# Half of a first-product sum goes through ScalarE into another PSUM bank, in 16 steps of a fused attention and FFN kernel

## The chip, the cores and the metric

The kernel runs on one core of a Trainium2 chip. The metric is device time in microseconds of one execution; the time given is the median of three runs. A core has TensorE (PE, matrix products, which write only to the accumulator memory PSUM), VectorE (DVE), ScalarE (ACT), GpSimd (POOL) and the queue engine SyncE (SP). Each engine works through its own list of instructions in the order in which the list is written, and waits at an instruction until what it needs from other engines has been signalled. PSUM has 8 banks, each of 128 partitions by 512 float32 values.

## What is computed

For each of B=4 batches, with q, k, v of 6080 x 256 values, a channel attention is computed, and on its output a feed-forward layer with an ELU:

```python
qn = q / (np.linalg.norm(q, axis=1, keepdims=True) + 1e-06)
kn = k / (np.linalg.norm(k, axis=1, keepdims=True) + 1e-06)
s = kn.transpose(0, 2, 1) @ qn / tau
a = softmax over the last axis of s          # 256 x 256 for each batch
x = (v @ a).reshape(24320, 256)
h = x @ w_in                                 # w_in: 256 x 2048
g = np.where(h > 0.0, h, np.exp(np.minimum(h, 0.0)) - 1.0)
out = g @ w_out                              # w_out: 2048 x 256
```

w_in and w_out come as float64.

## The kernel before

Since v @ a @ w_in = v @ (a @ w_in), the kernel forms W' = a @ w_in once for each batch (`wp_item`, tiles `wp`), so that two products are left for each piece of tokens: h = v W' (the first product) and out = g w_out (the second). To keep float32 accuracy on a faster matrix format, each operand is split into a high part and a low part, and each product is made of three matmuls: high x high, high x low, low x high.

The tokens lie along the columns. A batch has 6080 tokens in NB=12 chunks, eight of 512 and then four of 496, 48 chunks in all (numbered 0 to 47). The hidden dimension of 2048 is cut into FT=16 tiles f of 128. One **step** is one pair (chunk c, tile f). Chunks 0 to 3 go first in an interleaved order (64 steps); from chunk M=4 on, step 64 + (c - 4) x 16 + f is (c, f). Chunks 8 to 11, the last four of batch 0, are steps 128 to 191, with 496 columns each.

`take(i)` writes the instructions of step i:

- `h_item` (L416): the first product for step i, into `ph`, a PSUM tile of tag `w`. The contraction of 256 runs as KT=2 halves kt=0 and kt=1, three matmuls each (L423, L424, L425): six matmuls that add up in one bank.
- `elu` (L428): for odd f ScalarE makes a Relu of the negative and an exponential (L434, L435), and VectorE combines (L436); for even f ScalarE makes the exponential alone (L438) and VectorE does two operations (L439, L440). Both forms read `ph`.
- `split_g` (L443) for step i-1: ScalarE casts the high part of g, VectorE subtracts for the low part (L114, L115, the helper `split`).
- `out_item` (L455) for step i-3 (LAG = 3): the second product, six matmuls L461, L463, L465 for each of two output tiles, into the two tiles `po` of the chunk, which sum over all 16 f. Between them stand the matmuls of the next batch's q-k product (`gram`, L203 and L210) in some steps.
- after the last f of a chunk `store` (L468): ScalarE copies each `po` to SBUF (L487), and a DMA goes out on SP's queue (L489).
- side work: squares, casts and sums for the next batch's rows (L181, L114, L182; while batch 0 runs they are written behind steps 127, 131, 135 and so on to 159, among others), norms (step 166), the softmax, and the next batch's W' (`wp_item`).

**PSUM.** The 8 banks are given out by tag: `gram` 2, `w` WB=3 (`ph`, `pn`, `pt`, `pw`), and `o` 8 - KT - WB = 3 (the `po` tiles, two for each chunk). A tile holds its bank until the last instruction that uses it is done; the next tile of the tag waits for a free bank.

**What sets the order.** The framework traces the program and a planner writes each engine's list ahead of the run. Up to step 67 (`in_order`, L554 to L862) TensorE, VectorE and ScalarE are under a manual schedule: their lists have the order of the code. From then on the planner orders the instructions itself, with the order of the code as priority. Instructions in `side` are put behind the step's `elu` on their engine (`issue_after`).

Of the kernel before, what the change touches and what calls it, by code (L numbers as in the profile page):

```python
# [7 lines left out]
F32 = mybir.dt.float32  # L8
# [19 lines left out]
def in_turns(cols):  # L28

    if len(cols.shape) == 3:  # L30
        return cols.rearrange("p x (a b) -> p x b a", a=2)
    return cols.rearrange("p (a b) -> p b a", a=2)
# [22 lines left out]
def channel_attention_then_elu_ffn(ctx: ExitStack, tc, q, k, vT, tau, w_in, w_out, outT):  # L55
# [8 lines left out]
    nc = tc.nc  # L64
# [4 lines left out]
    P = 128  # L69
    KT = C // P  # L70
    FT = F // P
    DT = D // P
    CH = 512
# [14 lines left out]
                pieces.append((c, lo, lo + Q))  # L88
    WB = 3

    LINE = 2048
# [5 lines left out]
    ps = ctx.enter_context(tc.tile_pool(name="ps", bufs=4, space=bass.MemoryType.PSUM))  # L99
# [3 lines left out]
    ones_r = lead_pool.tile([P, P], F32R, name="ones_r")  # L103
# [7 lines left out]
    wo = const.tile([P, FT, 2, D], F32R, name="wo")  # L111
# [273 lines left out]
    def span(c):  # L385

        b, x = divmod(c, NB)
        return b, b * N + sum(sizes[:x]), sizes[x]
# [25 lines left out]
    wps = {}  # L414

    def h_item(c, f, vt):  # L416
        b, _, n = span(c)
        wp = wps[b]
        ph = ps.tile([P, CH], F32, tag="w", bufs=WB, name="ph")
        fs = slice(f * P, f * P + P)  # L420
        for kt in range(KT):
            hi, lo = (in_turns(vt[:, kt, x, 0:n]) for x in range(2))
            nc.tensor.matmul(ph[:, 0:n], wp[kt][:, 0, fs], hi, start=(kt == 0), stop=False)  # L423
            nc.tensor.matmul(ph[:, 0:n], wp[kt][:, 0, fs], lo, start=False, stop=False)  # L424
            nc.tensor.matmul(ph[:, 0:n], wp[kt][:, 1, fs], hi, start=False, stop=(kt == KT - 1))  # L425
        return ph

    def elu(c, ph, both):  # L428
        n = span(c)[2]
        e = work.tile([P, CH], F32, tag="e", bufs=3, name="e")  # L430
        ev, pv = e[:, 0:n], ph[:, 0:n]

        if both:
            nc.scalar.activation(ev, pv, AF.Relu, scale=-1.0)  # L434
            x = nc.scalar.activation(ev, ev, AF.Exp, scale=-1.0)  # L435
            y = nc.vector.scalar_tensor_tensor(ev, ev, -1.0, pv, op0=ALU.add, op1=ALU.max)  # L436
        else:
            x = nc.scalar.activation(ev, pv, AF.Exp)  # L438
            nc.vector.tensor_scalar(ev, ev, 1.0, -1.0, op0=ALU.min, op1=ALU.add)  # L439
            y = nc.vector.tensor_tensor(ev, pv, ev, op=ALU.max)  # L440
        return e, x, y

    def split_g(c, e):  # L443
        n = span(c)[2]
        g = work.tile([P, 2, CH], F32R, tag="g", bufs=4, name="g")
        split(g[:, 0, 0:n], g[:, 1, 0:n], e[:, 0:n])
        return g

    def first(c, f):
        return f == 0 or (c, f) in [(x, lo) for x, lo, _ in pieces]  # L450

    def last(c, f):
        return f == FT - 1 or (c, f) in [(x, hi - 1) for x, _, hi in pieces]

    def out_item(c, f, g, po, between):  # L455

        n = span(c)[2]
        hi, lo = (in_turns(g[:, x, 0:n]) for x in range(2))
        for dt in range(DT):
            o, ds = po[dt][:, 0:n], slice(dt * P, dt * P + P)  # L460
            nc.tensor.matmul(o, wo[:, f, 0, ds], hi, start=first(c, f), stop=False)  # L461
            next(between, None)
            nc.tensor.matmul(o, wo[:, f, 1, ds], hi, start=False, stop=False)  # L463
            next(between, None)
            nc.tensor.matmul(o, wo[:, f, 0, ds], lo, start=False, stop=last(c, f))  # L465
            next(between, None)

    def store(c, f, po):  # L468
        _, t0, n = span(c)
        ov = outT[:, t0 : t0 + n].rearrange("(k p) t -> p k t", p=P)  # L470
        if c < M:
            o = half[c]
        else:
            o = work.tile([P, DT, CH], F32, tag="o", bufs=1, name="o")
        for dt in range(DT):
            y, x = quarters(o[:, dt, 0:n]), quarters_of_turns(po[dt][:, 0:n])
            if c < M and (c, 0, f + 1) not in pieces:
                nc.vector.tensor_add(y, y, x)  # L478
            elif c == NCH - 1 and dt == DT - 1:

                m = n // 2
                nc.scalar.copy(y, x)
                nc.sync.dma_start(ov[:, dt, 0:m], o[:, dt, 0:m])
                nc.scalar.dma_start(ov[:, dt, m:n], o[:, dt, m:n])
                continue
            else:
                nc.scalar.copy(y, x)  # L487
            if f == FT - 1:
                nc.sync.dma_start(ov[:, dt], o[:, dt, 0:n])  # L489
# [53 lines left out]
    wi64, wo64, vraw, vts = {}, {}, {}, {}  # L543
    state = {}
# [228 lines left out]
    for b in range(1, B):  # L773
# [33 lines left out]
        for g in range(NG):  # L807
            x = s0 + length * g // NG
# [5 lines left out]
        x = s1 - FT - 6  # L814
# [18 lines left out]
    def take(i):  # L833

        if i < len(steps):
            c, f = steps[i]
            ph = h_item(c, f, vts[c])
            es[i], *done[:] = elu(c, ph, i < M * FT or f % 2 == 1)
        if 0 <= i - 1 < len(steps):
            gs[i - 1] = split_g(steps[i - 1][0], es.pop(i - 1))  # L840
        j = i - LAG
        if j >= 0:
            c, f = steps[j]
            if first(c, f):

                tag, bufs = ("o", 8 - KT - WB)
                if (c, f) in [piece[0:2] for piece in pieces[-2::-2]]:
                    tag, bufs = ("gram", KT)
                pos[c] = [ps.tile([P, CH], F32, tag=tag, bufs=bufs, name=f"po_{c}_{dt}") for dt in range(DT)]
            out_item(c, f, gs.pop(j), pos[c], fine.pop(i, iter(())))  # L850
            if last(c, f):
                store(c, f, pos.pop(c))
        for fn in loose.get(i, ()):
            fn()
        with tc.issue_after(done[0].ins), tc.issue_after(done[1].ins):
            for fn in side.get(i, ()):
                fn()

    done = []
    for i in range(M * FT + LAG):  # L860
        take(i)
    in_order.close()  # L862
    for i in range(M * FT + LAG, len(steps) + LAG):
        take(i)
# [31 lines left out]
```

## Time and profile before

| | |
|---|---|
| median of 3 runs | 2165.83 us |
| lowest, highest run | 2165.37, 2166.81 us |
| span of the profiled execution | 2163.4 us |
| granted TensorE clock, mean | 1.000 |
| idle before ScalarE's output copies L487, all 11 times | 5.4 us |
| start of step 128 in the trace (first matmul of chunk 8) | 409.38 us |
| start of step 132 | 420.85 us |

The profile comes from one execution, and its span runs from the first to the last instruction. In a timeline each row is start in us, duration in us, engine, line, operation, output <- inputs, shapes, and in brackets how long the engine had been idle and who released it. Matmuls overlap in the array: a duration of 0.37 us belongs to one whose successor starts 0.21 us later, so the spacing of the starts is what a matmul costs. PEld rows are weight loads, which run beside the matmul before. In a row of groups, the number behind x is the count, then come busy time and mean ns, then idle time before the group and its releasers.

### The profile page before, as it was taken

How to read it: one execution, taken by the hardware profiler on the slowest of the kernel's cores; microseconds unless marked ns; L12 is line 12 of the kernel's file. 1: busy time of each engine (PE TensorE's matmuls, PEld its weight loads, DVE VectorE, ACT ScalarE, POOL GpSimd, SP SyncE). 2: the span in 40 equal slices, each digit the busy share in tenths (PEclk: the TensorE clock that was granted, in tenths of full speed). 3: DMA queues.
4: the chain of work that ended last, by engine and by line, in shares of the span. 5: the costliest groups of instructions: out<-in, count | busy, mean ns of one | idle time of the engine just before them, and what ended most of it. 6: DMA issues, size and time to landing. Idle time of an engine off the chain costs nothing.

```text
span 2163.4 us, 27196 instructions
## 1 busy us (share of the span) xinstructions
PE 2158.6 (100%) x10240; PEld 1911.9 (88%) x10240; DVE 1527.0 (71%) x2358; ACT 1469.1 (68%) x2422; POOL 3.3 (0%) x11
## 2 busy tenths in 40 slices
PE   9999999999999999999999999999999999999999
PEld 8888888899888888889988888888998888888998
DVE  7987777778766776776776677667776666666665
ACT  6877777667666666666766666666776666666665
POOL 0000000000000000000000000000000000000000
PEclk9999999999999999999999999999999999999999
DMA  9320222221111111111111112111112000000000
GB/s 357 107 78 30 78 69 68 68 65 49 59 38 50 49 59 49 59 58 46 39 59 39 49 50 68 49 58 49 56 31 67 20 30 27 23 20 11 20 10 20
DMA packets 62532, 120.77 MB, mean 56 GB/s; under 512 B 6208, under 2 KB 16064, under 8 KB 62400
## 3 DMA queue, kind: packets, MB, share of 16 engines
q1 hardware_dynamic: 62256, 118.91, 16.6%
q8 instruction: 80, 1.31, 0.2%
q14 instruction: 52, 0.43, 0.1%
q10 hardware_dynamic: 144, 0.13, 0.0%
HBM read 92.01 MB, written 27.00 MB: 55 GB/s over the span
## 4 chain that ended last, share of the span: by engine, by line
PE 100%; ACT 0%; DVE 0%; issue 0%
PE po L465 15%; PE po L463 15%; PE ph L423 15%; PE po L461 15%; PE ph L424 15%; PE ph L425 15%; PE gram L203 3%; PE gram L549 2%; PE gram L210 1%; PE pw L374 1%; PE pw L373 1%; PE pw L375 1%; PE pe L549 0%; PE pw L370 0%; PE pd L222 0%; PE pt L337 0%
## 5 line engine op out<-in xcount | busy, mean ns | idle before, releaser
L114 ACT CAST g<-e 128x512 fp32r<-128x512 f32 (+1 forms) x768 | 469.6, 611 | 483.5 <-DVE e L440 281.6
L115 DVE TENSOR_TENSOR g<-e,g 128x512 fp32r<-128x512 f32 (+1 forms) x768 | 525.6, 685 | 323.0 <-ACT g L114 295.6
L465 PE MATMUL po<-g,wo 128*128 128x512 f32 (+1 forms) x1536 | 579.3, 377 | 0.0
L463 PE MATMUL po<-g,wo 128*128 128x512 f32 (+1 forms) x1536 | 579.2, 377 | 0.0
L461 PE MATMUL po<-g,wo 128*128 128x512 f32 (+1 forms) x1536 | 578.9, 377 | 0.0
L423 PE MATMUL ph<-vt,wp 128*128 128x512 f32 (+1 forms) x1472 | 555.4, 377 | 0.0
L425 PE MATMUL ph<-vt,wp 128*128 128x512 f32 (+1 forms) x1472 | 554.5, 377 | 0.0
L424 PE MATMUL ph<-vt,wp 128*128 128x512 f32 (+1 forms) x1472 | 554.5, 377 | 0.0
L436 DVE SCALAR_TENSOR_TENSOR e<-e,ph 128x512 f32<-128x512 f32 (+1 forms) x416 | 283.2, 681 | 242.5 <-ACT e L435 241.9
L434 ACT ACTIVATE e<-ph 128x512 f32<-128x512 f32 (+1 forms) x416 | 246.6, 593 | 129.1 <-PE ph L425 114.4
L461 PEld LDWEIGHTS po<-g,wo 128*128 128x128 f32 x1536 | 290.3, 189 | 37.9 <-DVE scr L478 0.2
L463 PEld LDWEIGHTS po<-g,wo 128*128 128x128 f32 x1536 | 290.3, 189 | 37.8
L465 PEld LDWEIGHTS po<-g,wo 128*128 128x128 f32 x1536 | 290.7, 189 | 34.8 <-DVE g L115 0.3
L424 PEld LDWEIGHTS ph<-vt,wp 128*128 128x128 f32 x1472 | 278.2, 189 | 36.2
L425 PEld LDWEIGHTS ph<-vt,wp 128*128 128x128 f32 x1472 | 278.2, 189 | 36.1
L423 PEld LDWEIGHTS ph<-vt,wp 128*128 128x128 f32 x1472 | 278.2, 189 | 36.1
L435 ACT ACTIVATE e<-e 128x512 f32<-128x512 f32 (+1 forms) x416 | 261.3, 628 | 12.6
L440 DVE TENSOR_TENSOR e<-ph,e 128x512 f32<-128x512 f32 (+1 forms) x352 | 240.6, 684 | 10.4
L438 ACT ACTIVATE e<-ph 128x512 f32<-128x512 f32 (+1 forms) x352 | 207.9, 591 | 31.1 <-PE ph L425 29.2
L439 DVE TENSOR_SCALAR e<-e 128x512 f32<-128x512 f32 (+1 forms) x352 | 147.0, 418 | 20.7 <-ACT e L438 20.6
L182 DVE TENSOR_TENSOR acc<-acc,sq 128x1024 f32<-128x1024 f32 x84 | 102.6, 1221 | 12.2 <-ACT sq L181 11.1
L203 PE MATMUL gram<-qk 128*128 128x512 f32 x268 | 101.6, 379 | 0.0
(134 smaller groups left out, 1183.1 us busy)
## 6 DMA issues: line engine op xcount, KB each, us to landing
raw<-in_q_dram SPq DMA_DIRECT2D x76, 256.0 KB, 2.7
raw<-in_k_dram SPq DMA_DIRECT2D x76, 256.0 KB, 3.0
v<-in_v_dram SPq DMA_DIRECT2D x32, 512.0 KB, 3.6
out_dram<-o SPq DMA_DIRECT2D x56, 256.0 KB, 2.1
v<-in_v_dram SPq DMA_DIRECT2D x16, 496.0 KB, 3.5
out_dram<-o SPq DMA_DIRECT2D x31, 248.0 KB, 2.1
wraw<-w_scr SPq DMA_DIRECT2D x12, 512.0 KB, 3.2
room<-in_q_dram SPq DMA_DIRECT2D x16, 256.0 KB, 5.2
```

The costliest lines, as they stand in the source:

```text
L114: nc.scalar.copy(hi, src)
L115: nc.vector.tensor_sub(lo, src, hi.bitcast(F32))
L423: nc.tensor.matmul(ph[:, 0:n], wp[kt][:, 0, fs], hi, start=(kt == 0), stop=False)
L424: nc.tensor.matmul(ph[:, 0:n], wp[kt][:, 0, fs], lo, start=False, stop=False)
L425: nc.tensor.matmul(ph[:, 0:n], wp[kt][:, 1, fs], hi, start=False, stop=(kt == KT - 1))
L434: nc.scalar.activation(ev, pv, AF.Relu, scale=-1.0)
L435: x = nc.scalar.activation(ev, ev, AF.Exp, scale=-1.0)
L436: y = nc.vector.scalar_tensor_tensor(ev, ev, -1.0, pv, op0=ALU.add, op1=ALU.max)
L440: y = nc.vector.tensor_tensor(ev, pv, ev, op=ALU.max)
L461: nc.tensor.matmul(o, wo[:, f, 0, ds], hi, start=first(c, f), stop=False)
L463: nc.tensor.matmul(o, wo[:, f, 1, ds], hi, start=False, stop=False)
L465: nc.tensor.matmul(o, wo[:, f, 0, ds], lo, start=False, stop=last(c, f))
```

## The change

In chunks 8 to 11, for f = 0, 4, 8 and 12 (16 steps), `h_item_seeded` takes the place of `h_item`. The three matmuls of kt=0 go into a tile `first_half` of tag `w`. ScalarE copies it into another bank, `seeded`, of tag `o`, and the three matmuls of kt=1 add to what the copy left there (no `start`). `seeded` is one tile for all 16 steps. Ahead of the first of them one matmul of ones with 512 columns of the weights is written into it. `elu` then reads `seeded` in place of `ph`. All other steps are as before.

```diff
+    SEEDED = (8, 12)
...
+    def h_item_seeded(c, f, vt):
+        b, _, n = span(c)
+        wp = wps[b]
+        if "seeded" not in state:
+            state["seeded"] = ps.tile([P, CH], F32, tag="o", bufs=8 - KT - WB, name="seeded")
+            nc.tensor.matmul(state["seeded"], ones_r, wo[:, 0].rearrange("p x d -> p (x d)"), start=True, stop=True)
+        first_half = ps.tile([P, CH], F32, tag="w", bufs=WB, name="first_half")
+        ph = state["seeded"]
+        fs = slice(f * P, f * P + P)
+        for kt in range(KT):
+            hi, lo = (in_turns(vt[:, kt, x, 0:n]) for x in range(2))
+            to, begin = (first_half, True) if kt == 0 else (ph, False)
+            end = kt == 0
+            nc.tensor.matmul(to[:, 0:n], wp[kt][:, 0, fs], hi, start=begin, stop=False, skip_group_check=not begin)
+            nc.tensor.matmul(to[:, 0:n], wp[kt][:, 0, fs], lo, start=False, stop=False, skip_group_check=not begin)
+            nc.tensor.matmul(to[:, 0:n], wp[kt][:, 1, fs], hi, start=False, stop=True, skip_group_check=not begin)
+            if kt == 0:
+                nc.scalar.copy(ph[:, 0:n], first_half[:, 0:n])
+        return ph
...
             c, f = steps[i]
-            ph = h_item(c, f, vts[c])
+            item = h_item_seeded if SEEDED[0] <= c < SEEDED[1] and f % 4 == 0 else h_item
+            ph = item(c, f, vts[c])
```

## The prediction, made before the changed kernel was run

> **What bounds the kernel now.** I read the page's span, busy shares and chain first, then the windows, then the timeline around steps that the change touches.
>
> ```profile
> span 2163.4 us, 27196 instructions
> ...
> PE 2158.6 (100%) x10240; PEld 1911.9 (88%) x10240; DVE 1527.0 (71%) x2358; ACT 1469.1 (68%) x2422; POOL 3.3 (0%) x11
> ...
> PEclk9999999999999999999999999999999999999999
> ...
> PE 100%; ACT 0%; DVE 0%; issue 0%
> ```
>
> TensorE is busy for 2158.6 of 2163.4 us, its clock is full in every slice, and the chain that ended last is made of matmuls. The three timed runs have their median at 2165.83 us, 2.43 us above the span of the profiled execution; I carry that difference over unchanged. So two things can move the time: the number of matmuls, and gaps between them. The other engines matter only where TensorE waits for them.
>
> ```profile
> 64.00:230.00 166.00, 166.00 (x771) 145.12 (x770) 140.37 (x201) 131.40 (x221) 0.00 (x0) 1.00 0.17 60
> ...
> 420.85:515.00 94.15, 94.15 (x466) 85.25 (x464) 69.64 (x105) 64.03 (x107) 0.68 (x1) 1.00 0.20 66
> ```
>
> These rows of the windows view give, after the length, the busy time of PE, weight loads, DVE, ACT and POOL, then clock, DMA share and GB/s. The second lies in the changed chunks: PE is busy all of it, ACT 64.03 of 94.15 us (68%).
>
> **The step, as it runs now.** The first product of step i is six matmuls (kt=0: L423, L424, L425; kt=1: the same), then six of the second product for step i-3. This is the timeline of step 136 (chunk 8, f=8), one of the 16:
>
> ```profile
> 431.69 1.04 ACT L181 ACTIVATE sq<-raw 128x1024 f32<-128x1024 f32 x1
> ...
> 432.20 0.37 PE L423 MATMUL ph<-vt,wp 128*128 128x496 f32 x1
> ...
> 432.62 0.37 PE L425 MATMUL ph<-vt,wp 128*128 128x496 f32 x1
> ...
> 432.64 1.03 ACT L114 CAST qk<-raw 128x1024 fp32r<-128x1024 f32 x1
> ...
> 432.83 0.37 PE L423 MATMUL ph<-vt,wp 128*128 128x496 f32 x1
> ...
> 433.46 0.37 PE L461 MATMUL po<-g,wo 128*128 128x496 f32 x1
> ...
> 433.57 0.60 ACT L114 CAST g<-e 128x496 fp32r<-128x496 f32 x1
> ...
> 434.08 0.57 ACT L438 ACTIVATE e<-ph 128x496 f32<-128x496 f32 x1
> ...
> 434.71 0.37 PE L423 MATMUL ph<-vt,wp 128*128 128x496 f32 x1
> ```
>
> Columns are start, duration, engine, line. Matmuls of 496 columns start 0.21 us apart. The kt=0 half's last matmul starts at 432.62, the kt=1 half follows at 432.83, the second product takes 433.46 to 434.71.
>
> **What the change adds.** Matmuls: the six stay six, with the same columns. One is new, once: `ones_r` times 512 columns, 0.22 us. Copies: 16 on ScalarE. Waits: the fourth matmul of a changed step needs the copy, and the copy needs the third matmul. Nothing is removed from TensorE, no DMA is added, SP's and POOL's queues are untouched. The nearest rows for the copy are those of the output copies, which read a PSUM bank and follow a matmul:
>
> ```profile
> L487 ACT COPY o<-po 128x496 f32<-128x496 f32 (+1 forms) x8 | 4.6, 575 | 1.0 <-PE po L465 0.9
> ```
> ```profile
> 416.91 0.59 ACT L487 COPY o<-po 128x512 f32<-128x512 f32 x1
> ...
> 417.47 0.38 PE L465 MATMUL po<-g,wo 128*128 128x512 f32 x1
> ...
> 417.89 0.59 ACT L487 COPY o<-po 128x512 f32<-128x512 f32 x1 [0.39 <-PE po L465]
> ...
> 418.94 0.37 PE L461 MATMUL po<-g,wo 128*128 128x496 f32 x1
> ...
> 420.11 0.37 PE L461 MATMUL po<-g,wo 128*128 128x496 f32 x1
> ```
>
> A copy takes 0.58 us; an idle ScalarE starts it 0.42 us after the start of the matmul it waits for (417.47 to 417.89). For the way back, this is an early step in which TensorE waits for VectorE:
>
> ```profile
> 65.55 0.68 DVE L115 TENSOR_TENSOR g<-e,g 128x512 fp32r<-128x512 f32 x1
> ...
> 66.28 0.19 PEld L465 LDWEIGHTS po<-g,wo 128*128 128x128 f32 x1 [0.30 <-DVE g L115]
> 66.28 0.48 PE L465 MATMUL po<-g,wo 128*128 128x512 f32 x1
> ...
> 66.60 0.38 PE L461 MATMUL po<-g,wo 128*128 128x512 f32 x1
> ```
>
> VectorE ends at 66.23, the weights load 0.05 us later, and the next matmul starts 0.32 us after the waiting one instead of 0.22: a wait that is felt costs 0.10 us more, because the weights were not loaded ahead.
>
> **Cost with nothing put in between.** With ScalarE free: 0.42 + 0.58 + 0.05 + 0.10 - 0.21 = 0.94 us of gap. In step 136 ScalarE is not free: the square (431.69) and the cast of rows (432.64) come from step 135 and hold it until 433.57, where the copy could start in place of the cast of g. It ends at 434.15, TensorE goes on at 434.20 where it now does at 432.83, and 0.10 for the weights makes 1.47 us. By the code, such row work is issued in steps 127, 131, ... 159, each just ahead of a changed step: 9 of the 16 pay 1.47, the other 7 pay 0.94. That is 13.2 + 6.6 = 19.8 us, the upper end.
>
> **What can hide it.** In step 136 six matmuls of the second product are ready meanwhile: their g is three steps old. Put in front of the kt=1 half they fill 432.83 to 434.08; one matmul of step 137's first product fills the slot to 434.29, later than 434.20. Nothing is left. With ScalarE free the copy ends at 433.62 and four of the six suffice. This is decided ahead of the run, by the order in which the planner writes TensorE's list, so I look for signs that it reorders. The first 67 steps stand under a manual order, the rest do not:
>
> ```profile
> 99.83 0.60 ACT L434 ACTIVATE e<-ph 128x512 f32<-128x512 f32 x1 [0.55 <-PE ph L425]
> 100.45 0.63 ACT L435 ACTIVATE e<-e 128x512 f32<-128x512 f32 x1
> 100.99 0.60 ACT L114 CAST g<-e 128x512 fp32r<-128x512 f32 x1
> ```
> ```profile
> 436.17 0.58 ACT L434 ACTIVATE e<-ph 128x496 f32<-128x496 f32 x1 [1.51 <-PE ph L425]
> 436.65 0.60 ACT L114 CAST g<-e 128x496 fp32r<-128x496 f32 x1
> 437.17 0.61 ACT L435 ACTIVATE e<-e 128x496 f32<-128x496 f32 x1
> ```
>
> The code writes L434, L435 and then L114. The manual part keeps that; the later part puts the cast between the two, at a point where it was ready and L435 was not. So ready work does overtake in the changed region. On TensorE I find no overtaking, but nothing there was ever blocked: this is the weak link. How good is the planned order in fact?
>
> ```profile
> 389.71 0.38 PE L425 MATMUL ph<-vt,wp 128*128 128x512 f32 x1
> ...
> 390.52 0.62 ACT L114 CAST g<-e 128x512 fp32r<-128x512 f32 x1 [2.01 <-DVE e L440]
> ...
> 391.05 0.59 ACT L434 ACTIVATE e<-ph 128x512 f32<-128x512 f32 x1
> ```
>
> L434 could have run at 389.71 + 0.42 = 390.13, yet ScalarE sat until 390.52 for a cast put first. The plan expected that cast at least 0.39 us sooner than it came. That is the largest such miss that I found. A plan that expects the copy too early puts too few matmuls in between, and TensorE waits for the difference plus 0.10. I take 0.10 us for each of the 16 steps, the price of a wait that is only just felt: some steps will have none, some a little more. The ends are 0 and 19.8 us.
>
> **The other edits.** The seeded bank is one of the three of tag `o`, held over chunks 8 to 11, so a new chunk's sums must wait until the old ones are copied out. The rows above cover that: the copies end at 417.50 and 418.48, the new sums start at 418.94 and 420.11, 1.44 and 1.63 us later. Cost 0; without that cover it is what the copies run late. The changed step's sum is complete later by up to 1.5 us, so g is late too:
>
> ```profile
> 437.29 0.68 DVE L115 TENSOR_TENSOR g<-e,g 128x496 fp32r<-128x496 f32 x1 [0.67 <-ACT g L114]
> ```
> ```profile
> 442.38 0.38 PE L465 MATMUL po<-g,wo 128*128 128x496 f32 x1
> ```
>
> Step 136's g is complete at 437.97 and its second part is first used at 442.38, 4.4 us of cover. Cost 0. Behind the copy in ScalarE's queue stand the cast of the step before and this step's exponential; 16 x 0.58 = 9.3 us on an engine that is 68% busy fits into its gaps. The tight place is the norms of batch 1, in step 167:
>
> ```profile
> 527.73 0.67 DVE L115 TENSOR_TENSOR g<-e,g 128x496 fp32r<-128x496 f32 x1
> ```
> ```profile
> 529.05 0.37 PE L465 MATMUL po<-g,wo 128*128 128x496 f32 x1
> ```
>
> There 0.65 us lie between 528.40 and 529.05, and step 168's copy may come ahead of that cast: 0.58 us, just covered.
>
> **The sum.** 0.22 + 16 x 0.10 = 1.8 us. Span 2163.4 + 1.8 = 2165.2; time 2165.83 + 1.8 = 2167.6 us.
>
> **Rivals.**
> Strict order: the planner leaves the kt=1 half right behind the copy's wait. 19.8 + 0.22 = 20.0 us, 2185.8 us. For it: in all steps of before TensorE's list is in the code's order. Against it: ScalarE's list is not. It decides from the point where fewer than four matmuls stand between the halves. The Trainium skill, TensorE: Matmul & The Clock Gate, section "Step-by-step: what each phase is for", says that TensorE itself pulls only weight loads ahead and keeps matmuls in program order. By that the chip would not repair a strict list, and the time would be this rival's; the wait at 66.28, with ready matmuls behind it, agrees.
>
> Plan too early everywhere: each step has the miss of 0.39 and the 0.10. 16 x 0.49 + 0.22 = 8.1 us, 2173.9 us.
>
> Banks: at the four chunk changes under the hold the output copy slips behind a changed copy, a square and a cast, 0.58 + 1.04 + 1.03 - 1.44 = 1.21 us each; with the 1.8, 6.6 us, 2172.4 us. Against it: no changed copy is issued in the same step as an output copy.
>
> Clock: the short gaps make the granted clock drop to half for the changed steps. Sixteen steps of 94.15 / 33 = 2.85 us (the window holds about 33 steps) would double: 45.6 us, 2211.4 us. Against it: with the wait at 66.28 the window 64 to 230 still reads 1.00. The same page of the Trainium skill, section "A second HAM failure mode: psum-queue depth-cycling", tells of short idle spells between groups of matmuls that made the clock swing between half and full; the trace shows none.
>
> That the second half overwrites the copy instead of adding to it would change the output, not the time: the same columns are written.
>
> Faster: TensorE has one matmul more and no gaps to lose, so only scatter remains.
>
> **How the numbers follow.** Nearly hidden 0.70 (2165.5 to 2170); plan too early 0.12; strict 0.12; banks 0.03; clock 0.01; faster 0.02. A change of 0.2% (4.3 us) is about what a measurement of this kernel tells from none. So same 0.70, slower 0.28, faster 0.02. The range 2164.8 to 2175 takes in the first two cases and the banks, 0.85.
>
> **What would show it.** Right: between the third and fourth first-product matmul of a changed step stand four to eight others, starts stay 0.21 us apart, ACT has 16 copies of about 0.58 us, the clock stays 1.00. Wrong: the fourth follows the third directly with a gap near 1 us and the copy as releaser (strict); gaps of 0.3 to 0.5 us with the same releaser (plan too early); gaps at the first sums of chunks 8 to 11 (banks).

## The result, and the profile after

| | before | after |
|---|---|---|
| median | 2165.88 us (18 runs) | 2169.88 us (18 runs) |
| lowest, highest | 2165.37, 2166.81 us | 2169.12, 2170.98 us |
| span of the profiled execution | 2163.4 us | 2168.0 us |

The ratio is 1.0018, with a 95% interval from 1.0011 to 1.0026: 4.0 us slower, just under the 0.2% that the prediction set as the bound of no change. The forecast was 1.8 us more. The interval leaves out 1: these runs do tell the 4.0 us from nothing, though the prediction reckoned that 0.2% is about what a measurement can tell.

These are the lines of the page after that answer to those shown of before. Lines of the code moved: the kt=0 half of a changed step is L443 to L445 on the tile `first_half`, its kt=1 half L443 to L445 on `seeded`, the copy L447, the second product L483, L485 and L487, the cast of `split` L116.

```profile
span 2168.0 us, 27209 instructions
...
PE 2161.1 (100%) x10241; PEld 1910.5 (88%) x10241; DVE 1529.6 (71%) x2358; ACT 1477.4 (68%) x2438; POOL 3.2 (0%) x11
...
PEclk9999999999999999999999999999999999999999
...
PE 97%; ACT 2%; issue 1%; DVE 0%; DMA 0%; SPq 0%; ACTq 0%
```

One matmul and 16 instructions of ScalarE more, the same full clock. The chain is no longer TensorE's alone: ACT has 2% and "issue" 1%. That share is not the loss, which is 0.2% of the span: where the chain goes back through a copy, it counts the square and the cast ahead of it too. The busy share hides the gaps, since it still reads 100%. The view of the tile `seeded` says who waits (here: duration min/median/max in ns, then first and last start):

```profile
L447 ACT COPY seeded<-first_half x16: 557/562/574, 411.0 to 586.1; 128x496 f32<-128x496 f32 x16
L443 PE MATMUL seeded<-vt,wp x16: 372/477/477, 411.6 to 586.8; 128*128 128x496 f32 x16
...
  ACT seeded L447: 6.9, 21
```

The 16 copies take 0.56 us each. The first matmul behind a copy lasts 0.477 us in the median instead of 0.372, the mark of a wait that is felt, as at 66.28 before. The last row sums the idle time of PE and of its weight queue behind the copy, so it counts some stretches twice.

Step 136 after, the one worked out in the prediction, in the timeline:

```profile
432.90 1.04 ACT L183 ACTIVATE sq<-raw 128x1024 f32<-128x1024 f32 x1
...
433.83 0.37 PE L445 MATMUL first_half<-vt,wp 128*128 128x496 f32 x1
...
433.85 1.03 ACT L116 CAST qk<-raw 128x1024 fp32r<-128x1024 f32 x1
...
434.04 0.37 PE L483 MATMUL po<-g,wo 128*128 128x496 f32 x1
...
434.79 0.56 ACT L447 COPY seeded<-first_half 128x496 f32<-128x496 f32 x1
434.88 0.37 PE L485 MATMUL po<-g,wo 128*128 128x496 f32 x1
...
435.40 0.19 PEld L443 LDWEIGHTS seeded<-vt,wp 128*128 128x128 f32 x1 [0.54 <-ACT seeded L447]
435.40 0.48 PE L443 MATMUL seeded<-vt,wp 128*128 128x496 f32 x1 [0.15 <-ACT seeded L447]
435.51 0.19 PEld L444 LDWEIGHTS seeded<-vt,wp 128*128 128x128 f32 x1
435.71 0.37 PE L444 MATMUL seeded<-vt,wp 128*128 128x496 f32 x1
```

The planner did reorder: five matmuls of the second product stand between the halves (434.04 to 434.88). The sixth came behind (a step's second product is six matmuls in all, three for each output tile). TensorE was free for the next at 434.88 + 0.21 = 435.09; the copy ended at 435.35 and the matmul started at 435.40. That is 0.31 us, and 0.10 more up to the next start (435.71 instead of 435.61). A step without row work ahead, later in the same trace:

```profile
537.06 0.37 PE L445 MATMUL first_half<-vt,wp 128*128 128x496 f32 x1
...
537.47 0.56 ACT L447 COPY seeded<-first_half 128x496 f32<-128x496 f32 x1 [0.65 <-PE first_half L445]
...
537.89 0.37 PE L483 MATMUL po<-g,wo 128*128 128x496 f32 x1
...
538.10 0.45 PE L443 MATMUL seeded<-vt,wp 128*128 128x496 f32 x1
...
538.39 0.37 PE L444 MATMUL seeded<-vt,wp 128*128 128x496 f32 x1
```

Here ScalarE was idle, the copy began 0.41 us after its matmul, four matmuls filled the time, and only 0.08 us were lost, to the weights (538.39 - 538.10 = 0.29 instead of 0.21).

By the spacing of the starts, the 16 steps lose: 9 behind row work 0.34 to 0.42 us each, 3.64 us together; 6 others 0.08 to 0.09 each, 0.48 us; step 168, which got ten matmuls in between, nothing. With the matmul of ones (0.22, and 0.02 at its border) that makes 4.4 us. The runs say 4.0, the spans 4.6.

### The profile page after: what moved, and what is told of

It reads as the page before. It is cut to its first block, busy times and chain, and to the rows that moved or that the text cites. A ratio compares the mean times of both kernels' runs of the same rounds, so it can differ in the third digit from the quotient of the medians.

```text
span 2168.0 us, 27209 instructions
## 1 busy us (share of the span) xinstructions
PE 2161.1 (100%) x10241; PEld 1910.5 (88%) x10241; DVE 1529.6 (71%) x2358; ACT 1477.4 (68%) x2438; POOL 3.2 (0%) x11
## 4 chain that ended last, share of the span: by engine, by line
PE 97%; ACT 2%; issue 1%; DVE 0%; DMA 0%; SPq 0%; ACTq 0%
PE po L487 15%; PE ph L425 15%; PE ph L427 15%; PE ph L426 15%; PE po L485 15%; PE po L483 15%; PE gram L205 2%; PE gram L571 2%; PE gram L212 1%; PE pw L377 1%; PE pw L375 1%; PE pw L376 1%; ACT sq L183 1%; PE pe L571 0%; ACT qk L116 0%
## 5 line engine op out<-in xcount | busy, mean ns | idle before, releaser
L116 ACT CAST g<-e 128x512 fp32r<-128x512 f32 (+1 forms) x768 | 469.5, 612 | 483.6 <-DVE e L462 282.9
L487 PE MATMUL po<-g,wo 128*128 128x512 f32 (+1 forms) x1536 | 579.3, 377 | 0.0
L485 PE MATMUL po<-g,wo 128*128 128x512 f32 (+1 forms) x1536 | 579.2, 377 | 0.0
L483 PE MATMUL po<-g,wo 128*128 128x512 f32 (+1 forms) x1536 | 578.9, 377 | 0.0
L425 PE MATMUL ph<-vt,wp 128*128 128x512 f32 (+1 forms) x1440 | 543.5, 377 | 0.0
L427 PE MATMUL ph<-vt,wp 128*128 128x512 f32 (+1 forms) x1440 | 542.6, 377 | 0.0
L426 PE MATMUL ph<-vt,wp 128*128 128x512 f32 (+1 forms) x1440 | 542.6, 377 | 0.0
L456 ACT ACTIVATE e<-ph 128x512 f32<-128x512 f32 (+1 forms) x416 | 246.6, 593 | 120.0 <-PE ph L427 105.3
L483 PEld LDWEIGHTS po<-g,wo 128*128 128x128 f32 x1536 | 290.3, 189 | 37.9 <-DVE scr L500 0.2
L485 PEld LDWEIGHTS po<-g,wo 128*128 128x128 f32 x1536 | 290.3, 189 | 37.8
L487 PEld LDWEIGHTS po<-g,wo 128*128 128x128 f32 x1536 | 290.7, 189 | 34.7 <-DVE g L117 0.3
L426 PEld LDWEIGHTS ph<-vt,wp 128*128 128x128 f32 x1440 | 272.2, 189 | 35.5
L427 PEld LDWEIGHTS ph<-vt,wp 128*128 128x128 f32 x1440 | 272.2, 189 | 35.5
L425 PEld LDWEIGHTS ph<-vt,wp 128*128 128x128 f32 x1440 | 272.2, 189 | 35.4
L462 DVE TENSOR_TENSOR e<-ph,e 128x512 f32<-128x512 f32 (+1 forms) x336 | 230.1, 685 | 10.2
L460 ACT ACTIVATE e<-ph 128x512 f32<-128x512 f32 (+1 forms) x336 | 198.6, 591 | 28.3 <-PE ph L427 26.5
```

What stands on the lines that cost most here:

```text
L116: nc.scalar.copy(hi, src)
```

## The experiments

The theory to test: the whole cost is TensorE's wait for the copy, and what hides it is only the number of matmuls that the list puts in between. The rivals: the copies as load on ScalarE, the bank taken from tag `o`, or the place of the steps in the kernel. Ratios are to the kernel before on the same chip (2165.67 us for e1 to e4, 2165.76 us for e5 to e8).

| experiment | median, us | over before, us | ratio, 95% interval |
|---|---|---|---|
| e1, list as written | 2186.03 | 20.36 | 1.0093 (1.0078 to 1.0109) |
| e8, before, list as written | 2165.80 | 0.04 | 1.0001 (0.9992 to 1.0010) |
| e4, copy of the whole sum | 2165.79 | 0.12 | 1.0000 (0.9992 to 1.0009) |
| e2, behind the second product | 2167.77 | 2.10 | 1.0010 (1.0001 to 1.0018) |
| e5, behind the next first product | 2166.08 | 0.32 | 1.0001 (0.9992 to 1.0010) |
| e3, two steps later | 2169.18 | 3.51 | 1.0016 (1.0007 to 1.0025) |
| e7, squares on VectorE | 2168.42 | 2.66 | 1.0013 (1.0004 to 1.0021) |
| e6, row work in halves | 2169.88 | 4.12 | 1.0019 (1.0011 to 1.0028) |

The intervals reach about 2 us to either side (3 in e1). By their times e1, e4 and e5 stand clear of the changed kernel; e2, e3 and e7 are told from it by the gaps in their traces alone. By the spacing of the starts the 16 steps lose 4.1 us in the changed kernel, 1.7 in e2, 3.2 in e3, 2.3 in e7, 4.0 in e6, and nothing in e4 and e5; the matmul of ones adds 0.24 to each.

### e1: the list as the code writes it

```diff
+    with tc.manual_schedule(engines={nc.tensor.engine}):
+        for i in range(M * FT + LAG, M * FT + 9 * FT):
+            take(i)
-    for i in range(M * FT + LAG, len(steps) + LAG):
+    for i in range(M * FT + 9 * FT, len(steps) + LAG):
         take(i)
```

> TensorE's list keeps the order of the code over steps 67 to 207, so nothing stands between the two halves of a changed step. Theory (the cost is TensorE's wait for the copy, and only what the planner put in between hides it): 9 steps behind row work wait 1.47 us each and 7 wait 0.94 us, with the matmul of ones 20.0 us over before, 2185.9 us, ratio 1.009. Rival (the 4 us of the change come from the 16 copies as load on ScalarE, the held bank or the matmul of ones, not from the wait): 2169.9 us as with the change.

It took 20.36 us more. Step 136 in its timeline:

```profile
436.48 0.37 PE L445 MATMUL first_half<-vt,wp 128*128 128x496 f32 x1
...
437.38 0.56 ACT L447 COPY seeded<-first_half 128x496 f32<-128x496 f32 x1
...
437.99 0.48 PE L443 MATMUL seeded<-vt,wp 128*128 128x496 f32 x1 [1.14 <-ACT seeded L447]
```

Nothing stands between the halves, and the next start comes 1.51 us after the third matmul instead of 0.21. The six ready matmuls of the second product stand behind the waiting one and do not pass it. That is the rule of the Trainium skill (TensorE: Matmul & The Clock Gate, "Step-by-step: what each phase is for") that matmuls stay in program order; this run agrees with it. So what the planner's reordering hid is measured too: 20.36 - 4.0 = 16.4 us.

### e8: the kernel before with the same manual order

The edit is that of e1, on the kernel before.

> The kernel before with the manual order on TensorE of the first experiment and nothing else. Theory: its list is the code's anyway, so the time is that of before within 0.1%, and all of the first experiment's 20 us belongs to the waits. Rival (the manual order has a price of its own): several us over before.

It took 0.04 us more, well inside the interval: the manual order itself has no price that these runs show, and e1's cost belongs to the waits.

### e4: all but the wait

```diff
-            to, begin = (first_half, True) if kt == 0 else (ph, False)
-            end = kt == 0
+            to, begin = first_half, kt == 0
...
-            if kt == 0:
-                nc.scalar.copy(ph[:, 0:n], first_half[:, 0:n])
+        nc.scalar.copy(ph[:, 0:n], first_half[:, 0:n])
```

> All six matmuls go into the first tile, and the copy moves the whole sum into the other bank, which the ELU reads: 16 copies, the held bank and the matmul of ones are all there, but no matmul waits for a copy. Theory of the wait: only the ones cost, 0.2 us, 2166.1 us and no gap in the 16 steps. Rival (load or bank): 2169.9 us.

```profile
L445 ACT COPY seeded<-first_half x16: 557/561/572, 411.5 to 582.7; 128x496 f32<-128x496 f32 x16
```

The 16 copies are there, the bank is held, and the time is that of before (0.12 us over). The starts of TensorE's matmuls show no gap that before does not have. Load on ScalarE, the third bank of tag `o` and the later sum have no price here.

### e2 and e5: more matmuls between the halves

In both, `h_item_seeded` makes one half for each call. In e2 the second is called behind `out_item` of the same step, in e5 behind `h_item` of the next, each with its `elu` behind it (the lines are those of e2):

```diff
+            later = SEEDED[0] <= c < SEEDED[1] and f % 4 == 0
+            if later:
+                h_item_seeded(c, f, vts[c], 0)
...
             out_item(c, f, gs.pop(j), pos[c], fine.pop(i, iter(())))
...
+        if i < len(steps) and later:
+            c, f = steps[i]
+            ph = h_item_seeded(c, f, vts[c], 1)
+            es[i], *done[:] = elu(c, ph, f % 2 == 1)
```

> The three matmuls of the second half are written behind the step's second product, so six matmuls stand between the halves in place of five or four. Theory of the wait: behind row work the copy comes 0.10 us after the six are issued, and the weights cost 0.10 more, 9 x 0.20; the other 7 steps pay nothing; with 0.22 for the ones 2.0 us over before, 2167.9 us. Rival (load or bank): 2169.9 us.

> The second half is written behind the first product of the next step, so twelve matmuls stand between the halves (2.5 us), and the sum is complete that much later. Theory of the wait: the copy is done long before, no gap in the 16 steps, 0.2 us over before for the ones, ratio 1.0001. Rival (the later sum makes g late, or the two-way use of the banks costs): gaps appear at the second product of the step three later, and the time stays 1 us or more above before.

e2 took 2.10 us more, where the wait gave 2.0; eight of the nine steps behind row work lose 0.21 us, and the first loses nothing. In its timeline (L446 on `seeded` is here the first matmul of the second half, L450 the copy) step 136 reads:

```profile
434.70 0.56 ACT L450 COPY seeded<-first_half 128x496 f32<-128x496 f32 x1
...
435.00 0.37 PE L490 MATMUL po<-g,wo 128*128 128x496 f32 x1
...
435.31 0.48 PE L446 MATMUL seeded<-vt,wp 128*128 128x496 f32 x1
435.62 0.37 PE L447 MATMUL seeded<-vt,wp 128*128 128x496 f32 x1
```

With six in between, 435.21 (435.00 + 0.21) is the free slot and 435.31 the start: 0.10, and 0.10 for the weights. e5 took 0.32 us more. With twelve to eighteen in between its second halves start 0.21 us behind the matmul before, and last what matmuls last without a wait:

```profile
L446 PE MATMUL seeded<-vt,wp x16: 372/372/373, 413.6 to 584.9; 128*128 128x496 f32 x16
```

All that is left of the cost is about the one matmul of ones, and the sum that is later by 2.5 us makes no g late. One or two matmuls more in a step bought 1.9 us of the change's 4.0 by the medians (2.4 by the traces), and six or more beyond that nearly all of the rest.

### e3 and e7: no row work, or less, ahead of the copy

```diff
-            item = h_item_seeded if SEEDED[0] <= c < SEEDED[1] and f % 4 == 0 else h_item
+            item = h_item_seeded if SEEDED[0] <= c < SEEDED[1] and f % 4 == 2 else h_item
```

> The changed steps are f = 2, 6, 10, 14 in place of 0, 4, 8, 12, so that no square and cast of rows stands right ahead of the copy on ScalarE. Theory (the plan comes too early only behind row work): all 16 steps have the short wait of 0.08 us, with the ones 1.5 us over before, 2167.4 us. Rival (the long waits belong to chunks 8 to 10 and not to the row work): nine waits of 0.42 us stay, 2169.9 us.

It took 3.51 us more, against 1.5 expected. The nine waits of 0.42 are gone: six of the nine early steps lose 0.17 us, two 0.31 and the first 0.27. So the place in time is not the cause. One of the six, with ScalarE idle ahead of the copy:

```profile
427.33 0.37 PE L445 MATMUL first_half<-vt,wp 128*128 128x496 f32 x1
...
427.74 0.56 ACT L447 COPY seeded<-first_half 128x496 f32<-128x496 f32 x1 [0.26 <-PE first_half L445]
...
428.17 0.27 PE L212 MATMUL gram<-qk 128*128 128x256 f32 x1
...
428.35 0.48 PE L443 MATMUL seeded<-vt,wp 128*128 128x496 f32 x1
```

The copy starts 0.41 us after its matmul, as early as in any step here, but the fourth matmul in between is one of 256 columns from the q-k product, which fills 0.11 us instead of 0.21: the free slot is at 428.28, and 0.07 and 0.10 are lost. The same four stand in eight of the early steps. The first has only three in between and waits 0.16 us, with ScalarE idle too. So the columns of the matmuls in between count, not their number alone. And of the seven later steps three lose 0.27 to 0.40 us, where in the changed kernel none of the later seven lost over 0.09. One of them:

```profile
540.38 0.59 ACT L116 CAST g<-e 128x496 fp32r<-128x496 f32 x1
...
540.65 0.37 PE L445 MATMUL first_half<-vt,wp 128*128 128x496 f32 x1
...
540.87 0.51 ACT L313 ACTIVATE a<-a,nm 128x256 f32<-128x256 f32 x1
...
541.38 0.56 ACT L447 COPY seeded<-first_half 128x496 f32<-128x496 f32 x1
541.49 0.37 PE L483 MATMUL po<-g,wo 128*128 128x496 f32 x1
...
541.99 0.48 PE L443 MATMUL seeded<-vt,wp 128*128 128x496 f32 x1
```

ScalarE is held there too, by the softmax's exponential (L313) and a cast, and the copy starts 0.73 us after its matmul instead of 0.41. The theory's word "only behind row work" falls: other work that holds ScalarE beyond the end of the first half does it too, where the list has too little in between. Step 168 of the changed kernel shows that condition: its copy started 1.08 us after its matmul, behind a cast and an exponential, and the ten matmuls in between hid it.

In e7 the squares of batch 1's rows move to VectorE:

```diff
-            square_rows(raw, state[b, "acc"], g == 0)
+            if b == 1 and g > 0:
+                sq = work.tile([P, 2, 2, C], F32, tag="sq", bufs=1, name="sq")
+                nc.vector.tensor_mul(sq, raw, raw)
+                nc.vector.tensor_add(state[b, "acc"], state[b, "acc"], sq)
+            else:
+                square_rows(raw, state[b, "acc"], g == 0)
```

> While batch 0 runs, the squares of rows are made by VectorE in place of ScalarE, so that ScalarE has only the cast of rows ahead of a copy and is done with it when the kt=0 half is complete. Theory (the long waits come from ScalarE being held by row work): the nine steps wait 0.08 us like the other seven, the first one about 0.3; with the ones 1.7 us over before. Rival (the place of the steps or the traffic of the banks): nine waits of 0.42 us stay, 4 us over before.

It took 2.66 us more, against 1.7 expected. Eight of the nine steps lose 0.19 us in place of 0.42, the first 0.27. The expected 0.08 was not reached because the cast of g slipped in ahead of the copy:

```profile
434.19 0.37 PE L445 MATMUL first_half<-vt,wp 128*128 128x496 f32 x1
434.20 0.60 ACT L116 CAST g<-e 128x496 fp32r<-128x496 f32 x1
...
434.71 0.56 ACT L447 COPY seeded<-first_half 128x496 f32<-128x496 f32 x1
...
435.03 0.37 PE L483 MATMUL po<-g,wo 128*128 128x496 f32 x1
...
435.32 0.48 PE L443 MATMUL seeded<-vt,wp 128*128 128x496 f32 x1
```

The copy started 0.52 us after its matmul, the list held four in between, and 0.08 + 0.10 was lost.

### e6: is it the wide instructions?

```diff
+                for t in range(2):
+                    nc.scalar.activation(sq[:, t], raw[:, t], AF.Square)
...
+                for t in range(2):
+                    nc.scalar.copy(hl[:, 0, t], raw[:, t])
```

> While batch 0 runs, the square and the cast of rows on ScalarE are two instructions of 512 columns each in place of one of 1024. The planner now puts six matmuls in place of five between the halves of eight of the nine steps behind row work. Theory A (the plan is too early only about the wide instructions): the copy is there in time, waits of 0.1 us or less, 16 x 0.08 and the ones, 1.5 us over before. Theory B (the plan is too early about any chain of instructions back to back on ScalarE): four halves take 0.18 us longer than two wholes, the copy comes 0.28 us after the six are issued, 0.38 us for each of the nine steps, 4.2 us over before, like the change.

It took 4.12 us more; theory B gave 4.2, theory A 1.5. The list held six matmuls in between instead of five, and the copy came later by as much:

```profile
435.24 0.56 ACT L447 COPY seeded<-first_half 128x496 f32<-128x496 f32 x1
435.35 0.37 PE L487 MATMUL po<-g,wo 128*128 128x496 f32 x1
...
435.85 0.48 PE L443 MATMUL seeded<-vt,wp 128*128 128x496 f32 x1
```

0.29 us and 0.10 again. So the width of the instructions is not it. If the planner adds matmuls until it takes the copy to be done, it expected the copy no later than the free slot and no more than one matmul (0.21 us) sooner. Then it was early by the wait at least, and by 0.21 us more at most: 0.31 to 0.52 us with the square and the cast, 0.29 to 0.50 with four halves, 0.08 to 0.29 with the cast of rows and the cast of g, and 0 to 0.21 where ScalarE was idle ahead of the copy. In e3 it was early with an idle ScalarE too, by 0.07 us at least in six steps and 0.16 in the first. So a planner that reckons ScalarE's work ahead of the copy shorter than it is would fit the four cases, but it is not all: the copy itself, the hand-over or the pace of the matmuls can be mis-timed as well. The planner's own times are in no trace, and which of them is off was not settled.

## Why the prediction was right, and what it mis-sized

- **What bounds the kernel**: right. TensorE's list sets the time, and e4 shows that 16 copies on an engine that is 68% busy cost nothing by themselves.
- **The cost with nothing in between**, 19.8 us and the ones: e1 measured 20.36, with 1.40 us for eight of the steps behind row work and 1.20 for the first (1.47 worked out), and 0.91 for five of the other seven (0.94). The two that are left cost 1.40 and 1.52, as ScalarE was held there too.
- **The planner fills the gap**: right. It was the weak link of the argument; the lists hold four or five matmuls of the second product in 15 of the 16 steps, where the prediction named six and one more for step 136.
- **How well it fills it**: this term was mis-sized. 16 x 0.10 = 1.6 us was taken; the trace shows 4.12 us, 3.64 in the nine steps behind row work. The 0.10 held for the other seven (0.08 or nothing). The prediction had the right size in hand, 0.39 us + 0.10 from the row at 390.52, and put it on all 16 steps or on none. The view of before shows what it missed, where that row stands:

```profile
387.74 1.22 DVE L115 TENSOR_TENSOR qk<-raw,qk 128x1024 fp32r<-128x1024 f32 x1
```

  This is row work in VectorE's queue, ahead of the two operations that the late cast waited for, so the miss that the prediction quoted stood behind row work already; no run tests whether that is why the plan missed there. With 0.49 for the nine and 0.08 for the seven the sum would have been 5.2 us, with the sign of the error reversed but nearer to 4.0.
- **The cover for banks and g**: right. e4 and e5 show no gap there.
- **The rivals**: strict order is what e1 built, at 2186.03 us against 2185.8 worked out. "Plan too early" came true for nine steps of 16, with 0.34 to 0.42 in place of 0.49. Banks and clock did not happen: there is no gap at the first sums of chunks 8 to 11, and the granted clock is 1.000.
- **Same, slower**: the measured 0.18% lies within the bound of 0.2% set for "same", its interval reaches over it. That the time falls into "nearly hidden" (up to 2170 us) by 0.12 us, and into "same" by 0.3 us, is luck: the cost was more than twice the forecast, and the nine waits are the sign that the prediction had set for "plan too early".

## What to carry to other kernels

A hand-over from TensorE to ScalarE and back takes about 1 us here (0.91 us of gap in e1 where ScalarE was free), and is nearly free as long as the list holds that much other work between the two halves; count the matmuls in between with their columns, and count what ScalarE has ahead of the copy. Where a planner writes the list, do not trust its count to the last matmul: e5, with the second half written one first product later, left 0.3 us, about the matmul of ones, while the planner's own place left 4 us. None of the versions beats the kernel before, since nothing is taken off TensorE.

## What the runs showed of the hardware

A copy of 496 columns from one PSUM bank to another took 0.557 to 0.574 us, 0.562 in the median; the 31 output copies of 496 columns from PSUM to SBUF before have a mean of 0.573 us, which is inside that spread. A wait that ends late costs TensorE more than its length: in the nine steps behind row work the matmul behind it lasts 0.477 us and the next start comes 0.31 us after it, 0.10 more than usual, about a quarter of their loss. In the six others that lose time the next start comes 0.29 to 0.30 us after it, and that is all of their loss.
